# One-core attention, mixing and gated product on Trainium2: d's two halves as even and odd numbers

## The chip, the cores and the metric

The kernel runs on one core of a Trainium2 chip. The metric is the time of the whole program on the device, in microseconds (us). TensorE (PE) multiplies and writes to PSUM; each of its matrix products comes with a load of the stationary tile, which the profile lists as an engine of its own (PEld). VectorE (DVE), ScalarE (ACT) and GpSimd (POOL) do the elementwise work. SP's queue issues most DMAs, POOL's the others.

## The reference, cut to what matters

```python
# attention: u, v are (4, 3072, 256), z is (4, 3072, 64)
attn = np.maximum((z @ z.T) / S, 0) ** 2
x = u * (attn @ v)
# mixing with the row before, then a gated net of width 1024
x_prev = x shifted down by one row, zeros in the first
xk = mu_k * x + (1 - mu_k) * x_prev
xr = mu_r * x + (1 - mu_r) * x_prev
k = np.maximum(xk @ w_k, 0)
x = sigmoid(xr @ w_r) * (k * k @ w_v)
# a second gated product of width 1536
out = ((x @ w_a) * (x @ w_b)) @ w_out
```

The large weights come as float64, so the device reads them as pairs of 32-bit words and decodes them. mu_k and mu_r have one number for each of the 256 columns d of x.

## The kernel before

The program has three stages. In the first, attention, there are 24 blocks of 512 rows (4 batches of 6), and each is worked through in 12 pairs of key tiles. For a pair, two products make scores (`sc`, lines 461 and 462), ScalarE squares them (lines 474 and 475), or a block that was kept earlier is read back from DRAM (`pm`, line 506), since the scores are symmetric. Then the squared scores are split into a rounded part `hi` and a rest `lo` (lines 520, 522, 523). v is split in the same way into `vhi` and `vlo`. Three products per tile, `vhi*hi`, `vhi*lo` and `vlo*hi`, are summed in PSUM by `mm3` (lines 102 to 104) into two accumulators `acc[0]` and `acc[1]`, each of 128 columns of d by 512 rows. The inner function `bb` of `summed` picks v's stationary tile: `vh[:, k, c]` with `c = slice(d * P, (d + 1) * P)`, so half d holds columns 128 d to 128 d + 127, which lie side by side. Everything is in float32 or its rounded form for TensorE.

u is needed with d on the partitions. `u_load` (line 435) brings a block of 512 rows as 32-row squares in eight DMAs of 64 KB on SP's queue, each with runs of 32 numbers, and `u_prep` (line 441) turns the squares with one VectorE transpose for each half. `result` multiplies the accumulators by u, `change` and `mixed` make xk and xr, which go to DRAM for the second stage.

The second stage (`mixture1`) is the first gated net, by a scheme with seven products of half-size blocks in place of eight, and the third (`mixture2`) the second product by the same scheme. Weights are decoded during attention (`decode`), in steps that stand beside the attention's units; their rows are put on partitions by the views in `chunks` and `rows`.

The order is written out by hand: a list of units, and beside it a list of side steps with the number of the unit at which each stands (`at`). The u load of a block stands 4 units into the block, its two transposes 12 and 14 units in. In the second batch and after, v's parts come by GpSimd's DMAs (`v_parts`, lines 412 and 419): `vhi` is cast by the DMA, ScalarE writes its negative to `vlo` (line 416), and a second DMA adds v to that. Five pools of tiles hold the buffers; `ust`, `raw` and others share three (`stp`).

Of the kernel before, what the change touches and what calls it, by code (L numbers as in the profile page):

```python
# [8 lines left out]
F32 = mybir.dt.float32  # L9
# [6 lines left out]
P = 128  # L16
QB = 512
SQ = 32
# [10 lines left out]
def tile_kernel(  # L29
# [29 lines left out]
    nc = tc.nc  # L59
# [4 lines left out]
    ND = D // P  # L64
# [10 lines left out]
    stp = ctx.enter_context(tc.tile_pool(name="stp", bufs=3))  # L75
# [13 lines left out]
    mu = const.tile([P, 2, ND], F32, name="mu")  # L89
    edge = const.tile([P, ND], F32, name="edge")  # L90

    def g_tile(shape, dtype, name):
        return gp.tile(shape, dtype, tag="g", name=name)
# [7 lines left out]
    def mm3(ps, wh, wl, ah, al, first, last):  # L101
        nc.tensor.matmul(ps, wh, ah, start=first, stop=False)  # L102
        nc.tensor.matmul(ps, wh, al, start=False, stop=False)  # L103
        nc.tensor.matmul(ps, wl, ah, start=False, stop=last)  # L104
# [9 lines left out]
    def at(i, fn):  # L114
        sides.setdefault(max(i, 0), []).append(fn)
# [203 lines left out]
    def z_load(b, s, t=None, queues=()):  # L319


        if t is None:
            t = zp.tile([P, QB // SQ, SQ], F32, tag="zn", name="zn")
        for n in range(2):
            src = z[b, (s + n) * QB : (s + n + 1) * QB, :].rearrange("(b i) (a j) -> a i b j", i=SQ, j=SQ)
            for a in range(DK // SQ):
                c = n * DK + a * SQ
                (queues[a] if queues else nc.sync).dma_start(t[c : c + SQ], src[a])
        zn_t[b, s] = t

    def z_prep(b, s):

        n = s % 2
        h, l = (slice(m * DK, (m + 1) * DK) for m in (n, 1 - n))

        def turn():
            t = zt_t[b, s] = zt_t[b, s + 1] = ztp.tile([P, QB], F32, tag="zt", name="zt")
            raw = zn_t.pop((b, s)).rearrange("p b j -> p (b j)")
            if b or s:
                nc.vector.transpose(t, raw)  # L340
            else:
                nc.vector.transpose(t[:DK], raw[:DK])
                return lambda: nc.vector.transpose(t[DK:], raw[DK:])

        def high():
            kt_t[b, s] = ktp.tile([P, QB], F32R, tag="kt", name="kt")
            if b or s < 2:
                nc.scalar.activation(kt_t[b, s][h], zt_t[b, s][h], AF.Copy)
            else:
                nc.vector.tensor_copy(kt_t[b, s][h], zt_t[b, s][h])  # L350

        def low():
            nc.vector.tensor_tensor(kt_t[b, s][l], zt_t[b, s][h], kt_t[b, s][h].bitcast(F32), op=ALU.subtract)

        return turn, high, low
# [9 lines left out]
    def q_prep(b, s):  # L365


        def half(h):
            kt = kt_t[b, s].bitcast(F32)
            if h == 0:  # L370
                q_t[b, s] = g_tile([P, 2, QB], F32R, "q")
            q = q_t[b, s]
            m = h ^ s % 2
            k = turned_order(kt[m * DK : (m + 1) * DK])
            nc.vector.tensor_copy(by_order(q[0:DK, h, :]), k)
            nc.scalar.activation(by_order(q[DK : 2 * DK, h, :]), k, AF.Copy)

        return lambda: half(0), lambda: half(1)
# [6 lines left out]
    def v_load(s):  # L385
        vst_t[s] = g_tile([P, TPB, D], F32, "vst")
        nc.sync.dma_start(vst_t[s], v_rows(0, s))
# [34 lines left out]

    ust_t, ut_t = {}, {}

    def by_squares(rows, i):


        r = rows[i * QB : (i + 1) * QB, :]
        return r.rearrange("(b i) (h a j) -> a i h b j", i=SQ, h=ND, j=SQ)

    def u_load(i):
        t = stp.tile([P, ND, QB // SQ, SQ], F32, tag="st", name="ust")
        for d in range(ND):
            for a, src in enumerate(by_squares(u.rearrange("b s d -> (b s) d"), i)):
                nc.sync.dma_start(t[a * SQ : (a + 1) * SQ, d], src[:, d])
        ust_t[i] = t

    def u_prep(i, d):
        if d == 0:
            ut_t[i] = g_tile([P, ND, QB], F32, "ut")  # L440
        nc.vector.transpose(ut_t[i][:, d, :], ust_t[i][:, d].rearrange("p b j -> p (b j)"))

    early_z = []
    x_kept, p_kept = {}, {}
# [1 line left out]
    def attention(i):  # L446
        b, qb = divmod(i, NQB)
        base = len(units)
        acc = {}
# [46 lines left out]
        def mirrored(kb, pr):  # L496

            st = {}

            def load():  # L500
                if pr:
                    return
                m = pm_t[kb] = pmp.tile([P, TPB, TPB, P], F32, tag="pm", name="pm")
                rows = p_kept[b, qb, kb].rearrange("(a q) (g c) t i -> g q a (c t i)", q=SQ, g=TPB)
                for g in range(TPB):
                    nc.sync.dma_start(m[g * SQ : (g + 1) * SQ].rearrange("q a c r -> q a (c r)"), rows[g])

            def a():
                st["p"] = halves(pm_t[kb][:, :, 2 * pr : 2 * pr + 2, :].rearrange("p a t r -> p t a r"), True)

            return st, a, load
# [14 lines left out]
        def summed(st, kb, pr, first, last):  # L526
            def bb():
                if first:
                    for d in range(ND):
                        acc[d] = accp.tile([P, QB], F32, tag="acc", name="acc")  # L530
                hi, lo = st["p"]
                vh, vl = v_t[b, kb]
                for t in range(2):
                    k = 2 * pr + t
                    for d in range(ND):
                        c = slice(d * P, (d + 1) * P)
                        mm3(
                            acc[d], vh[:, k, c], vl[:, k, c], hi[:, t, :], lo[:, t, :],
                            first and t == 0, last and t == 1,
                        )  # L540

            return bb

# [37 lines left out]
        for n, fn in enumerate(steps):  # L581
            t = base + NKT + (2 * AHEAD + 3 * n + 3 if i < NB - 1 else n + 4)
# [4 lines left out]
        if qb == 0:  # L587
            for s in range(0 if b else 1, NQB):
                need = base + s * TPB
                turn, high, low = z_prep(b, s)  # L590
                if b:
                    w = base - 16 + (s - NQB + 2) * NKT - 8 * (s < NQB - 1)
# [24 lines left out]
        for n, (_, m, kb, pr) in enumerate(order):  # L617
            if m:
                st, a, load = mirrored(kb, pr)
                at(base + 2 * n - 9, load)  # L620
            else:
                st, a = scored(kb, pr, base + 2 * n)
# [758 lines left out]
    n2 = len(units)  # L1381
    mixture2()

    chunks = [(("r", 0), 0, w_r.rearrange("(k p) d -> p k d", p=P))]
    def by_rows(name, w, g):
        wr = w.rearrange("(n t p) d -> n p t d", p=P, t=2)
        for h in range(2):
            chunks.append(((name, g), h * QB, wr[2 * g + h]))
# [3 lines left out]
    place = iter([  # L1392
        (DEC1 if b else DEC0) + n * DEC + b * NQB * NKT for b in range(B) for n in range(PER if b else PER - 1)
    ])
    rows = {n: w.rearrange("(k p) f -> k p f", p=P) for n, w in (("a", w_a), ("b", w_b), ("k", w_k))}
    groups = [("s", (g,), ("b", g), ("a", g)) for g in range(NF2 // TPB)] + [("k", (), ("k", 1), ("k", 0))]
    for kind, g, low_rows, high_rows in groups:
        val = {}
# [14 lines left out]
        i = next(place)  # L1413
# [30 lines left out]
    with tc.manual_schedule():  # L1444
        z_load(0, 0, None, (nc.sync, nc.scalar))
        zs = g_tile([P, 2, QB // SQ, SQ], F32, "zs")
        z_load(0, 2, zs[:, 0])
        v_load(0)
        z_load(0, 4, zs[:, 1])
        for n in range(1, NQB):  # L1450
            v_load(n)
        for c, m in enumerate((mu_k, mu_r)):
            nc.sync.dma_start(mu[:, c, :], m.rearrange("(d p) -> p d", p=P))
        turn, high, low = z_prep(0, 0)
        turn_next = turn()
        for fn in (high, low, *q_prep(0, 0), turn_next, *early_z[0]):
            fn()
        for n, fn in enumerate(v_split(0)):
            at(n // 2, fn)
        last = max(len(units), max(sides) + 1)  # L1460
        for i in range(last):
            if i == n1:
                while pending:
                    pending.popleft()()
                early.close()
                late["ps"] = ctx.enter_context(
                    tc.tile_pool(name="psp", bufs=4, space=bass.MemoryType.PSUM, reuse_waits="tile")
                )
                late["w"] = ctx.enter_context(tc.tile_pool(name="wp", bufs=6, reuse_waits="tile"))
                late["p"] = ctx.enter_context(tc.tile_pool(name="late", bufs=18, reuse_waits="tile"))  # L1470
            for fn in sides.get(i, ()):
                fn()
            if i < len(units):
                a, b, ahead = units[i]
                if a is not None:
                    a()
                if b is not None:
                    pending.append(b)
            else:
                ahead = 0  # L1480
            while len(pending) > ahead:
                pending.popleft()()
# [27 lines left out]
```

## Time and profile before

| | before |
|---|---|
| median of 3 runs (range) | 2548.71 us (2547.96 to 2548.97) |
| the profiled execution, its own time | 2548.83 us |
| its span, first to last instruction | 2546.9 us |
| PE busy | 2529.3 us, 11128 products |
| PEld busy | 2089.4 us, 11128 loads |
| DVE busy | 2055.2 us |
| ACT busy | 1848.8 us |
| DMA | 335842 packets, 495.22 MB; 189056 packets under 512 B |

A product's mean duration in the profile, near 390 ns, runs from the issue to the modelled end, and products overlap in it. What each costs in a dense stretch is the distance from one start to the next, or the count of products over the length of a stretch. Attention takes the first 950 us or so, the second stage some 500 us, the third the rest.

### The profile page before, as it was taken

To read this page: it belongs to the slowest core of one execution; us is meant where nothing else is said; L and a number is where in the kernel's file an instruction comes from. 1 tells how busy PE (TensorE), PEld (TensorE's weight loads), DVE (VectorE), ACT (ScalarE), POOL (GpSimd) and SP (SyncE) were. 2 spreads that over 40 slices of the span, in tenths; PEclk is the share of its full clock that TensorE was granted. 3 is DMA by queue.
4 is the path that set the end of the run, shared out by engine and by line. 5 is a ranking of instruction groups with operands and counts; after the bars stand their busy time and mean duration, and the time that the engine had idled before them with its cause. 6 is when DMAs were issued, how large, how long until landed. Compare 5 with 4: busy or idle time off the path is not lost.

```text
span 2546.9 us, 32165 instructions
## 1 busy us (share of the span) xinstructions
PE 2529.3 (99%) x11128; PEld 2089.4 (82%) x11128; DVE 2055.2 (81%) x2879; ACT 1848.8 (73%) x2519; POOL 372.2 (15%) x382
## 2 busy tenths in 40 slices
PE   8999999999999999999999999999999999999999
PEld 6887888888888888888888888888888888888887
DVE  9997999799979886666666668888888888888887
ACT  7865987687687758888888876666666666666665
POOL 0111211210120100000000002222222222212211
PEclk9999999999999999999999999999999999999999
DMA  8789888997997793112122146666766676666664
GB/s 215 223 234 237 261 252 232 249 281 224 243 257 233 227 264 141 67 58 92 50 75 75 50 144 245 194 235 199 240 196 231 212 223 207 223 227 217 213 194 137
DMA packets 335842, 495.22 MB, mean 194 GB/s; under 512 B 189056, under 2 KB 211584, under 8 KB 328000
## 3 DMA queue, kind: packets, MB, share of 16 engines
q1 hardware_dynamic: 293232, 362.75, 49.4%
q0 software_dynamic: 40848, 129.77, 15.7%
q8 instruction: 87, 1.43, 0.2%
q10 hardware_dynamic: 1600, 0.66, 0.1%
q14 instruction: 75, 0.61, 0.1%
HBM read 357.04 MB, written 136.05 MB: 194 GB/s over the span
## 4 chain that ended last, share of the span: by engine, by line
PE 94%; DVE 2%; issue 1%; DMA 1%; ACT 1%; POOL 0%; SPq 0%; DVEq 0%; POOLq 0%
PE px L992 15%; PE acc L103 9%; PE acc L104 9%; PE acc L102 9%; PE py L992 8%; PE px L715 5%; PE oacc L1023 4%; PE oacc L1021 4%; PE oacc L1022 4%; PE pw L992 4%; PE vacc L102 3%; PE vacc L104 3%; PE vacc L103 3%; PE py L715 3%; PE sc L461 2%; PE sc L462 2%
## 5 line engine op out<-in xcount | busy, mean ns | idle before, releaser
L103 PE MATMUL acc<-lo,vhi 128*128 128x512 f32 x1152 | 449.3, 390 | 1.4 <-DVE lo L523 1.4
L102 PE MATMUL acc<-hi,vhi 128*128 128x512 f32 x1152 | 449.1, 390 | 0.8 <-DVE hi L522 0.8
L104 PE MATMUL acc<-hi,vlo 128*128 128x512 f32 x1152 | 448.9, 390 | 0.0
L992 PE MATMUL px<-t,sw 128*128 128x512 f32 x1296 | 364.1, 389 | 0.0
L992 PEld LDWEIGHTS px<-t,sw 128*128 128x128 f32 x1296 | 243.2, 188 | 50.7 <-DVE cc L1177 0.3
L103 PEld LDWEIGHTS acc<-lo,vhi 128*128 128x128 f32 x1152 | 216.7, 188 | 48.0 <-DVE lo L523 2.9
L102 PEld LDWEIGHTS acc<-hi,vhi 128*128 128x128 f32 x1152 | 216.6, 188 | 46.3 <-DVE hi L522 1.2
L104 PEld LDWEIGHTS acc<-hi,vlo 128*128 128x128 f32 x1152 | 216.6, 188 | 44.8
L1077 ACT ACTIVATE pw<-px 128x512 f32<-128x512 f32 x144 | 83.8, 582 | 197.8 <-PE px L992 197.8
L474 ACT ACTIVATE p<-sc 128x1024 f32<-128x1024 f32 x167 | 169.6, 1016 | 57.2 <-PE sc L462 56.5
L1189 POOL TENSOR_TENSOR cc<-cc 128x512 f32<-128x512 f32 x72 | 93.1, 1293 | 804.8 <-DVE b L1043 581.8
L523 DVE TENSOR_TENSOR lo<-p,hi 128x1024 fp32r<-128x1024 f32 x167 | 199.5, 1195 | 4.2
L1089 DVE TENSOR_TENSOR u<-py,u 128x512 f32<-128x512 f32 x144 | 99.5, 691 | 124.8 <-PE py L992 124.8
L475 ACT ACTIVATE p<-p 128x1024 f32<-128x1024 f32 x167 | 177.3, 1062 | 5.3
L481 DVE STREAM_TRANSPOSE pt<-p 128x512 f32<-128x512 f32 x240 | 155.5, 685 | 28.9 <-ACT p L475 27.5
L523 DVE TENSOR_TENSOR lo<-pm,hi 128x1024 fp32r<-128x1024 f32 x120 | 145.7, 1215 | 27.8 <-ACT hi L520 27.6
L1132 ACT ACTIVATE c<-pw 128x512 f32<-128x512 f32 x144 | 86.4, 600 | 111.0 <-PE pw L992 81.3
L520 ACT ACTIVATE hi<-pm 128x1024 fp32r<-128x1024 f32 x120 | 124.4, 1050 | 45.5 <-DMA pm<-pkept 35.1
L1187 POOL TENSOR_TENSOR cc<-cc 128x512 f32<-128x512 f32 x71 | 91.8, 1293 | 438.9 <-DVE bl L1043 218.3
L102 PE MATMUL vacc<-kh,w 128*128 128x512 f32 x384 | 149.4, 389 | 0.0
L104 PE MATMUL vacc<-kh,w 128*128 128x512 f32 x384 | 149.4, 389 | 0.0
L103 PE MATMUL vacc<-kl,w 128*128 128x512 f32 x384 | 149.4, 389 | 0.0
(213 smaller groups left out, 6051.2 us busy)
## 6 DMA issues: line engine op xcount, KB each, us to landing
sw<-kept SPq DMA_DIRECT2D x252, 512.0 KB, 5.5
pkept<-pt POOLq DMA_DIRECT2D x60, 1024.0 KB, 6.0
pm<-pkept SPq DMA_DIRECT2D x240, 256.0 KB, 6.6
ow<-kept SPq DMA_DIRECT2D x120, 512.0 KB, 6.7
kept<-w POOLq DMA_DIRECT2D x42, 512.0 KB, 5.4
ust<-in_u SPq DMA_DIRECT2D x192, 64.0 KB, 5.7
xkept<-xr POOLq DMA_DIRECT2D x24, 512.0 KB, 7.0
xkept<-xk POOLq DMA_DIRECT2D x24, 512.0 KB, 6.3
```

Of the source, the lines that this page charges most:

```text
L102: nc.tensor.matmul(ps, wh, ah, start=first, stop=False)
L103: nc.tensor.matmul(ps, wh, al, start=False, stop=False)
L104: nc.tensor.matmul(ps, wl, ah, start=False, stop=last)
L474: nc.scalar.activation(p, sc, AF.Relu, scale=1.0 / S)
L475: nc.scalar.activation(p, p, AF.Square)
L481: nc.vector.transpose(pt[:, :, 2 * pr + t, :], p[:, t, :].rearrange("p (c i) -> p c i", i=SQ))
L520: nc.scalar.activation(h, p, AF.Copy)
L523: nc.vector.tensor_tensor(l, p, h.bitcast(F32), op=ALU.subtract)
L715: nc.tensor.matmul(bank, w[x][:, c], t[:, y, :], start=first and m == 0, stop=end and m == 2, skip_group_check=True)
L992: nc.tensor.matmul(bank, w, t[:, y, :], start=first and m == 0, stop=end and m == 2, skip_group_check=True)
L1021: nc.tensor.matmul(acs[bank], wh, hi, start=first, stop=False, skip_group_check=True)
L1022: nc.tensor.matmul(acs[bank], wl, hi, start=False, stop=False, skip_group_check=True)
```

## The change

Half d of the 256 columns was columns 128 d to 128 d + 127; it is now the columns 2 j + d, so half 0 holds the even and half 1 the odd ones. Four things follow.

- u's block is loaded in four DMAs of 128 KB with runs of 64 numbers (256 bytes) in place of eight with runs of 32, and the transposes of a half read every second number of `ust`.
- v's stationary tiles `vh` and `vl` are read by TensorE with a stride of two numbers. v itself is stored as before.
- mu's view is `(p d)` in place of `(d p)`.
- The rows of w_r and w_k are put on partitions as `(p k)` in place of `(k p)`, so that a partition has the two neighbouring rows.

The products, the VectorE, ScalarE and GpSimd instructions and their order are the same, row for row; on SP's queue the u loads have four DMAs each. The shapes of mu's two loads and of w_r's one change too. On SP, at the start of the program (`vst` is v, `ust` u, `zn` z, `pm` kept scores), before:

```order
L387 DMA vst<-in_v 128x4x256 x5
L1453 DMA mu<-in_moe_mu_k 128x2x1
L1453 DMA mu<-in_moe_mu_r 128x2x1
L435 DMA ust<-in_u 32x16x32 x8
L328 DMA zn<-in_z 32x16x32 x4
L506 DMA pm<-pkept 32x4x512 x4
```

and with the change:

```order
L387 DMA vst<-in_v 128x4x256 x5
L1444 DMA mu<-in_moe_mu_k 128x2
L1444 DMA mu<-in_moe_mu_r 128x2
L429 DMA ust<-in_u 32x16x64 x4
L328 DMA zn<-in_z 32x16x32 x4
L499 DMA pm<-pkept 32x4x512 x4
```

What stood behind a u load stands behind four DMAs in place of eight, and nothing changes places.

```diff
-    def by_squares(rows, i):
-        r = rows[i * QB : (i + 1) * QB, :]
-        return r.rearrange("(b i) (h a j) -> a i h b j", i=SQ, h=ND, j=SQ)
-
     def u_load(i):
-        t = stp.tile([P, ND, QB // SQ, SQ], F32, tag="st", name="ust")
-        for d in range(ND):
-            for a, src in enumerate(by_squares(u.rearrange("b s d -> (b s) d"), i)):
-                nc.sync.dma_start(t[a * SQ : (a + 1) * SQ, d], src[:, d])
-        ust_t[i] = t
+        t = ust_t[i] = stp.tile([P, QB // SQ, ND * SQ], F32, tag="st", name="ust")
+        r = u.rearrange("b s d -> (b s) d")[i * QB : (i + 1) * QB]
+        for a, src in enumerate(r.rearrange("(b i) (a c) -> a i b c", i=SQ, c=ND * SQ)):
+            nc.sync.dma_start(t[a * SQ : (a + 1) * SQ], src)
 
     def u_prep(i, d):
         if d == 0:
             ut_t[i] = g_tile([P, ND, QB], F32, "ut")
-        nc.vector.transpose(ut_t[i][:, d, :], ust_t[i][:, d].rearrange("p b j -> p (b j)"))
+        nc.vector.transpose(ut_t[i][:, d, :], ust_t[i].rearrange("p b (j h) -> p h b j", h=ND)[:, d])
...
                     for d in range(ND):
-                        c = slice(d * P, (d + 1) * P)
-                        mm3(
-                            acc[d], vh[:, k, c], vl[:, k, c], hi[:, t, :], lo[:, t, :],
-                            first and t == 0, last and t == 1,
-                        )
+                        h, l = (x[:, k, :].rearrange("p (c h) -> p h c", h=ND)[:, d] for x in (vh, vl))
+                        mm3(acc[d], h, l, hi[:, t, :], lo[:, t, :], first and t == 0, last and t == 1)
...
-    chunks = [(("r", 0), 0, w_r.rearrange("(k p) d -> p k d", p=P))]
+    chunks = [(("r", 0), 0, w_r.rearrange("(p k) d -> p k d", p=P))]
...
-    rows = {n: w.rearrange("(k p) f -> k p f", p=P) for n, w in (("a", w_a), ("b", w_b), ("k", w_k))}
+    rows = {n: w.rearrange("(k p) f -> k p f", p=P) for n, w in (("a", w_a), ("b", w_b))}
+    rows["k"] = w_k.rearrange("(p k) f -> k p f", p=P)
...
-            nc.sync.dma_start(mu[:, c, :], m.rearrange("(d p) -> p d", p=P))
+            nc.sync.dma_start(mu[:, c, :], m.rearrange("(p d) -> p d", p=P))
```

## Rows read from the trace of the kernel before

**Rows 1.** The page: busy time by engine; granted TensorE clock and DMA in slices.
```profile
PE 2529.3 (99%) x11128; PEld 2089.4 (82%) x11128; DVE 2055.2 (81%) x2879; ACT 1848.8 (73%) x2519; POOL 372.2 (15%) x382
PEclk9999999999999999999999999999999999999999
DMA  8789888997997793112122146666766676666664
```
**Rows 2.** PE's waits: who waited for whom, us in total, times, longest.
```profile
PE sc L461 <- DVE q L375: 6.4, 1, 6.4
PE sc L461 <- ACT p L474: 3.2, 2, 2.4
PE acc L103 <- DVE lo L523: 1.4, 2, 0.8
PE acc L102 <- DVE hi L522: 0.8, 1, 0.8
```
**Rows 3.** Stretches of the span: busy us (instructions) of PE, PEld, DVE, ACT, POOL; clock, DMA.
```profile
100.00:200.00 100.00, 100.00 (x443) 82.84 (x442) 94.09 (x141) 72.51 (x82) 11.10 (x18) 1.00 0.86 233
200.00:300.00 100.00, 97.58 (x430) 80.47 (x430) 78.68 (x114) 73.09 (x78) 21.00 (x25) 1.00 1.11 252
...
1800.00:2300.00 500.00, 500.00 (x2207) 414.17 (x2206) 419.12 (x572) 334.75 (x537) 118.20 (x93) 1.00 0.66 216
```
**Rows 4.** Groups by line: count, busy us, mean ns, idle before. Products, then loads.
```profile
L103 PE MATMUL acc<-lo,vhi 128*128 128x512 f32 x1152 | 449.3, 390 | 1.4 <-DVE lo L523 1.4
...
L103 PEld LDWEIGHTS acc<-lo,vhi 128*128 128x128 f32 x1152 | 216.7, 188 | 48.0 <-DVE lo L523 2.9
```
**Rows 5.** Timeline at 249 us, attention: start, duration in us; products, then loads.
```profile
249.01 0.39 PE L102 MATMUL acc<-hi,vhi 128*128 128x512 f32 x1
249.24 0.39 PE L103 MATMUL acc<-lo,vhi 128*128 128x512 f32 x1
...
249.01 0.19 PEld L103 LDWEIGHTS acc<-lo,vhi 128*128 128x128 f32 x1
249.24 0.19 PEld L104 LDWEIGHTS acc<-hi,vlo 128*128 128x128 f32 x1
```
**Rows 6.** Timeline at 20 us, where the clock is low for a while.
```profile
20.48 0.63 PE L104 MATMUL acc<-hi,vlo 128*128 128x512 f32 x1
20.90 0.63 PE L102 MATMUL acc<-hi,vhi 128*128 128x512 f32 x1
...
20.48 0.33 PEld L102 LDWEIGHTS acc<-hi,vhi 128*128 128x128 f32 x1
```
**Rows 7.** The transposes at the end (moving side 128 columns): timeline; durations min/median/max in ns.
```profile
2540.32 0.36 PEld L1344 LDWEIGHTS pt<-one,ot 128*128 128x128 f32 x3
...
L1344 PEld LDWEIGHTS pt<-one,ot x16: 138/140/143, 2539.2 to 2540.9; 128*128 128x128 f32 x16
```
**Rows 8.** Groups on DVE, as in rows 4.
```profile
L182 DVE TENSOR_SCALAR e<-raw 128x512 uint32<-128x512 uint32 x27 | 11.3, 418 | 0.2
...
L470 DVE CAST hi<-p 128x512 fp32r<-128x512 f32 x2 | 0.8, 420 | 0.0
...
L441 DVE STREAM_TRANSPOSE ut<-ust 128x512 f32<-128x512 f32 x48 | 33.9, 705 | 0.6
```
**Rows 9.** Timelines of 225 to 256 us: SP's queue, ACT, PE; idle before in brackets.
```profile
225.20 17.01 SPq L435 DMA_DIRECT2D ust<-in_u  x8
...
250.94 1.06 ACT L416 ACTIVATE vlo<-vhi 128x1024 fp32r<-128x1024 f32 x1 [5.12 <-DMA vhi<-in_v]
...
252.96 0.50 PE L461 MATMUL sc<-q,kt 128*128 128x512 f32 x1 [2.42 <-ACT p L474]
```
**Rows 10.** u's DMAs; SP's queue in 13:60, then 1130:1230: packets, MB, share of 16 engines.
```profile
ust<-in_u SPq DMA_DIRECT2D x192, 64.0 KB, 5.7
...
q1 hardware_dynamic: 13998, 5.90, 58.7%
...
q1 hardware_dynamic: 2752, 6.29, 18.0%
```

## The prediction

> **What bounds the kernel now.** I read the page's busy times first, then PE's waits, then stretches by count of products, and last single products and loads. PE is busy for 2529.3 of the span's 2546.9 us, at a granted clock that shows nine tenths or more in all forty slices [rows 1]. Busy alone proves little, since products overlap in the record, so the count decides: 443 products in 100 us of attention, 2207 in 500 us of the third stage [rows 3]. That is 225.7 and 226.6 ns from one start to the next in two stages whose other engines and DMAs are loaded quite differently (a DMA share of 0.86 and 0.66). So the spacing is PE's own, and 11128 products at 226.6 ns make 2521.6 us of the span.
>
> What is left for others to give back is small. PE's waits with a releaser sum to 6.4 + 3.2 + 1.4 + 0.8 = 11.8 us [rows 2]. 6.4 is the start, before the first operand is there. Of the rest, the single wait of 0.8 for `hi` and the longest, 0.8, of the two for `lo` come before 20 us; what stays later is the 3.2 us for ScalarE's `p` and 0.6 us for `lo`, 3.8 us in all. The largest single piece is a hole of 2.42 us that ends at 252.96 us [rows 9]. The stretch 200 to 300 us shows it: 430 products where 443 fit, 13 x 226 ns = 2.9 us [rows 3].
>
> **The change part by part.** *v's stationary tiles.* It touches the loads of lines 102 to 104 in attention: 3 x 1152 = 3456 of them, each 188 ns, each beside a product [rows 4]. Only the load's reading changes; the product's moving side stays contiguous. A load starts with the product before its own (both at 249.01, then both at 249.24) [rows 5] and is followed by (48.0 - 2.9) us / 1152 = 39 ns in which the load side has nothing to do [rows 4]. So a load may grow by 39 ns before anything is late. How much of a load is reading is seen in the transposes at the end, which move only 128 columns and so don't hide their loads: three loads of 140 ns stand in 0.36 us, hence (360 - 140) / 2 = 110 ns from one to the next at full clock [rows 7]. No row shows TensorE reading with a stride. The nearest row is VectorE: `raw` is read in every second 32-bit word at line 182, 418 ns for 512 words, and the contiguous cast of 512 float32 at line 470 takes 420 ns [rows 8]. That stride costs nothing there, at VectorE's faster rate of the two in these rows. By this row the cost is 0; at the other end, with reading at half the rate, a load takes 188 + 110 = 298 ns, 298 - 188 - 39 = 71 ns too long, and 3456 x 0.071 = 245 us. A gain is excluded: the spacing of 226 ns is the same with contiguous tiles everywhere, and a stride takes no work away. I take 0, the value of the nearest row, and price the other end as a rival.
>
> [...]
>
> *u's loads.* 192 DMAs of 64 KB become 96 of 128 KB, and a block's 8 x 512 = 4096 packets of 128 bytes become 2048 of 256. The price of a packet I fit to two stretches of SP's queue [rows 10]: 13998 packets of 421 bytes in the mean took 58.7% of 16 engines for 47 us, 441 us or 31.5 ns each; 2752 of 2286 bytes took 18.0% for 100 us, 288 us or 104.7 ns each. That is 0.039 ns a byte, so 20 ns at 128 bytes and 25 ns at 256, an estimate. A block's u takes 4096 x 20 / 16 = 5.1 us of all engines now and 2048 x 25 / 16 = 3.2 us then: 1.9 us less, 24 times, 46 us of DMA time. Nearly all of it is hidden under PE's products. Where it isn't is the hole at 250 us: SP is occupied for 17.01 us from 225.20 with one u load, against a median of 5.7 us to landing for such a DMA, in a stretch where the DMA queues together show 1.11 of 16 engines; ScalarE's negative of v then waits 5.12 us for `vhi`'s DMA, and the scores' `p` behind it on ScalarE holds PE for 2.42 us [rows 3, 9, 10]. I take 1.9 us of these 2.42 back. The bounds are a gain of all 3.8 us and a loss of 2.4 us, another hole of that size, since the kept scores, z and raw weights behind u on SP's queue now start sooner and may meet v's DMAs elsewhere.
>
> *u's transposes.* 48 of 705 ns, now reading with a stride of two [rows 8]. Taken at 0 by line 182's row; at the other end they double, 48 x 0.705 = 34 us of VectorE work (priced below). The cover is VectorE's idle time: 5.9 us in the stretch 100 to 200, 21 us in 200 to 300 [rows 3]. Each half's first transpose now needs four DMAs that bring both halves, not its own four; the load stands eight units ahead, which is more than the landing time.
>
> *mu, w_r, w_k, and the waits.* Two loads of 1 KB, one of 512 KB and four of 512 KB keep their places and sizes; w_r's runs become longer. What waits for them is decoding and mixing far behind on VectorE and ScalarE. 0, with 0.5 us either way.
>
> The sum: 2548.83 (the profiled execution, 0.12 above the median) + 0 - 1.9 + 0 + 0 = 2546.9 us.
>
> **The rivals.** *The load becomes the bound.* It decides once a strided load takes over 188 + 39 = 227 ns. For it: the load cannot start before the product ahead of it does, so a longer load shows at once [rows 5]. Against it: line 182's row, and even at half rate 220 ns from load to load would still fit in 227 if only the rate counted. Price up to 245 us, 2546.9 + 245 = 2792 us; slower. Chance 0.10.
>
> [...] Chance 0.08.
>
> *VectorE becomes late.* If the strided transposes take twice as long, some of the 34 us come through where VectorE is full: about half of the 24 blocks, 0.7 us each, 8 us, 2555 us. PE waited for VectorE only 0.6 us after 20 us, so the cover is mostly there. Chance 0.04.
>
> *The DMAs give back more than PE's recorded waits.* A gain of over 0.2% is 5.1 us, more than the 3.8 us that PE loses after 20 us; it would need a shorter start too, which u has no part in. 2543 us, chance 0.02.
>
> *The larger packets do nothing* (SP's DMAs still collide with v's): 2548.8 us. This lies within the forecast.
>
> **How the numbers follow.** The forecast, strided reading free and a small relief of the DMAs, has 0.76, between 2545 (all 3.8 us back) and 2551.3 (a second hole). 0.2% is about what a measurement of this kernel can tell from no change, so it counts as the same. Slower is 0.10 + 0.08 + 0.04 = 0.22, faster 0.02, the same 0.76. The range of 2543 to 2556 us takes in the forecast, the faster case and VectorE's, 0.82 less a little at the forecast's own edges; the two TensorE rivals are left out.
>
> **What would show it.** Right: the loads of lines 102 to 104 still at 188 ns, 443 products in 100 us of attention, the u transposes at 705 ns, packets under 512 bytes down from 189056 by some 49000, and a shorter hole near 250 us. [...] The forecast is wrong if the spacing in attention is no longer that of the third stage.

## The result: 0.8% slower, in the products with v

| | before | after |
|---|---|---|
| median (range) | 2548.84 us (2547.96 to 2550.35) | 2568.53 us (2568.1 to 2568.68) |
| ratio, 95% interval | | 1.0076 (1.0059 to 1.0094) |
| span of the profiled execution | 2546.9 us | 2566.9 us |

The changed kernel's page begins with the busy time by engine, and further down gives the packets:

```profile
PE 2551.4 (99%) x11128; PEld 2108.9 (82%) x11128; DVE 2056.7 (80%) x2879; ACT 1850.1 (72%) x2519; POOL 372.5 (15%) x382
...
DMA packets 284770, 495.21 MB, mean 193 GB/s; under 512 B 138112, under 2 KB 160640, under 8 KB 276928
...
ust<-in_u SPq DMA_DIRECT2D x96, 128.0 KB, 7.5
```

PE's waits after the change (who waited for whom, us in total, times, longest):

```profile
PE sc L454 <- DVE q L375: 6.4, 1, 6.4
PE acc L102 <- DVE hi L515: 1.1, 1, 1.1
PE acc L103 <- DVE lo L516: 1.0, 2, 0.8
PE sc L454 <- ACT p L461: 0.3, 1, 0.3
PE acc L103 <- DVE lo L464: 0.2, 1, 0.2
PE sc L454 <- DVE kt L353: 0.2, 1, 0.2
```

Two stretches by engine (PE, PEld, DVE, ACT, POOL; then clock and DMA), one of attention and one of the third stage:

```profile
100.00:200.00 100.00, 100.00 (x431) 82.94 (x430) 91.03 (x136) 71.81 (x81) 10.79 (x17) 1.00 0.85 225
...
1800.00:2300.00 500.00, 500.00 (x2208) 414.32 (x2207) 418.52 (x573) 333.42 (x534) 118.19 (x93) 1.00 0.67 220
```

And groups of the products with v, their loads and u's transposes (count, busy us, mean ns, idle before):

```profile
L103 PE MATMUL acc<-lo,vhi 128*128 128x512 f32 x1152 | 455.5, 395 | 1.5 <-DVE lo L516 1.0 <-DVE lo L464 0.2
...
L103 PEld LDWEIGHTS acc<-lo,vhi 128*128 128x128 f32 x1152 | 223.1, 194 | 49.2 <-DVE lo L516 4.1 <-DVE lo L464 0.5
...
L434 DVE STREAM_TRANSPOSE ut<-ust 128x512 f32<-128x512 f32 x48 | 33.9, 706 | 2.3 <-DMA ust<-in_u 1.2 <-issue 0.8
```

Read against [rows 2 to 4, 8, 10]: the third stage runs as before, 2208 products for 2207. Attention at the full clock runs 431 products where 443 ran, with PE busy for all 100 us of both. PE doesn't wait more; it waits less, 9.2 us in all for 11.8, and the hole of 2.4 us is gone. The loads of v's tiles grew by only 6 ns, from 188 to 194, and still have their idle time of near 40 ns each, and nonetheless every product came later. The transposes are as fast as they were.

Between 600 and 950 us, where PE waits for nothing in either kernel, the count gives the size (all lines, columns as above):

```profile
600.00:950.00 350.00, 350.00 (x1546) 289.93 (x1545) 308.03 (x460) 252.40 (x284) 45.07 (x66) 1.00 0.91 238
...
600.00:950.00 350.00, 350.00 (x1507) 290.17 (x1506) 305.44 (x459) 255.51 (x287) 45.47 (x67) 1.00 0.88 233
```

The first line is before, the second after: 350 / 1545 = 226.5 ns and 350 / 1506 = 232.4 ns from start to start. 1279 of the 1507 are products with v; put down to them alone, each costs (232.4 - 226.5) x 1506 / 1279 = 6.9 ns more. Read one by one in the trace, the starts of successive products with v stand 233.3 ns apart in this stretch, 226.7 before, so 6.7 ns. The scores' products between them, whose own tiles lie side by side in both kernels, come a little later as well (228.0 ns from one to the next, 226.7 before). At 6.7 ns, the size that the products alone show below too, 3456 products make 23.2 us; less the 2.6 us that PE waits less, 20.6 us, for a difference of spans of 20.0 us.

### The profile page after: what moved, and what is told of

Same layout as the page of the kernel before. It is cut to its first block, busy times and chain, and to the rows that moved or that the text cites. A ratio compares the mean times of both kernels' runs of the same rounds, so it can differ in the third digit from the quotient of the medians.

```text
span 2566.9 us, 32030 instructions
## 1 busy us (share of the span) xinstructions
PE 2551.4 (99%) x11128; PEld 2108.9 (82%) x11128; DVE 2056.7 (80%) x2879; ACT 1850.1 (72%) x2519; POOL 372.5 (15%) x382
## 3 DMA queue, kind: packets, MB, share of 16 engines
q0 software_dynamic: 40848, 129.77, 15.5%
## 4 chain that ended last, share of the span: by engine, by line
PE 95%; DVE 2%; issue 1%; DMA 1%; SPq 0%; POOL 0%; ACT 0%; DVEq 0%; POOLq 0%; ACTq 0%
PE px L982 15%; PE acc L103 9%; PE acc L104 9%; PE acc L102 9%; PE py L982 8%; PE px L705 5%; PE oacc L1013 4%; PE oacc L1011 4%; PE oacc L1012 4%; PE pw L982 4%; PE vacc L102 3%; PE vacc L104 3%; PE vacc L103 3%; PE py L705 3%; PE sc L455 3%; PE sc L454 3%
## 5 line engine op out<-in xcount | busy, mean ns | idle before, releaser
L103 PE MATMUL acc<-lo,vhi 128*128 128x512 f32 x1152 | 455.5, 395 | 1.5 <-DVE lo L516 1.0
L102 PE MATMUL acc<-hi,vhi 128*128 128x512 f32 x1152 | 454.8, 395 | 1.1 <-DVE hi L515 1.1
L104 PE MATMUL acc<-hi,vlo 128*128 128x512 f32 x1152 | 454.7, 395 | 0.0
L103 PEld LDWEIGHTS acc<-lo,vhi 128*128 128x128 f32 x1152 | 223.1, 194 | 49.2 <-DVE lo L516 4.1
L102 PEld LDWEIGHTS acc<-hi,vhi 128*128 128x128 f32 x1152 | 223.2, 194 | 47.4 <-DVE hi L515 1.5
L104 PEld LDWEIGHTS acc<-hi,vlo 128*128 128x128 f32 x1152 | 223.1, 194 | 45.4
```

## Experiments

### One half of the change each: u_only, v_only

u_only is the changed kernel with v's tiles side by side again; u's loads and transposes and the views of mu, w_r and w_k stay changed:

```diff
-                        h, l = (x[:, k, :].rearrange("p (c h) -> p h c", h=ND)[:, d] for x in (vh, vl))
-                        mm3(acc[d], h, l, hi[:, t, :], lo[:, t, :], first and t == 0, last and t == 1)
+                        c = slice(d * P, (d + 1) * P)
+                        mm3(
+                            acc[d], vh[:, k, c], vl[:, k, c], hi[:, t, :], lo[:, t, :],
+                            first and t == 0, last and t == 1,
+                        )
```

> The changed kernel with v's stationary tiles read side by side again, as before; u's 256-byte packets, the strided transposes and the other views stay, so that the halves of d no longer match and the product with u mixes columns. If the strided loads are the whole loss: about 2546.5 us, between 2545 and 2548.7, loads of lines 102 to 104 back at 188 ns and 443 products in 100 us of attention. If u's loads or the strided transposes have part in the loss: over 2551 us.

Measured: 2552.76 us against 2549.32, ratio 1.0009 (1.0000 to 1.0018). The signs of the first case came back, 443 products in 100 us and loads of 188 ns:

```profile
100.00:200.00 100.00, 100.00 (x443) 82.81 (x442) 94.17 (x141) 72.82 (x82) 11.39 (x18) 1.00 0.87 234
...
L104 PEld LDWEIGHTS acc<-hi,vlo 128*128 128x128 f32 x1152 | 216.2, 188 | 44.6
```

Its time did not: the median lies over the 2551 us that stood for a part of u in the loss. Against the kernel before, run beside it, the difference is 0 to 4.6 us by the interval. So a small part of the 20 us may belong to what u_only keeps changed, and a gain of 1.9 us isn't there.

v_only is the kernel before with this edit the other way round: v's tiles with a stride of two, nothing else.

> The kernel before with v's stationary tiles read with a stride of two, nothing else, so that the halves of d no longer match u's. If the strided loads are the whole loss: 3456 loads x 6 ns = 21 us, 2569 to 2570 us, a little over the changed kernel since the hole near 250 us stays. If u has part in it: under 2560 us.

Measured: 2568.15 us against 2549.32, ratio 1.0071 (1.0057 to 1.0085): the loss of the whole change, within the intervals. Between 600 and 950 us it runs the same 1507 products as the changed kernel, and its PE waits keep the hole (2.5 us for `p`), as expected:

```profile
600.00:950.00 350.00, 350.00 (x1507) 289.31 (x1506) 305.69 (x460) 254.16 (x286) 45.52 (x67) 1.00 0.89 234
...
PE sc L461 <- ACT p L474: 2.5, 1, 2.5
```

The stride of v's stationary tiles is the cause of the loss.

This run also shows strided tiles at the lower clock: the granted clock was 0.50 from 19.2 to 22.4 us. There the products stand 0.42 to 0.43 us apart, as they do without a stride [rows 6], so no cost of the stride shows at that clock:

```profile
19.54 0.63 PE L104 MATMUL acc<-hi,vlo 128*128 128x512 f32 x1
19.97 0.63 PE L102 MATMUL acc<-hi,vhi 128*128 128x512 f32 x1
20.39 0.63 PE L103 MATMUL acc<-lo,vhi 128*128 128x512 f32 x1
```

u_only also shows where the relief of the DMAs went. SP's queue is done with the u load at 225 us in 5.79 us, not 17.01 [rows 9]; these are the rows of its timeline (SP, then ACT), and of its PE waits:

```profile
225.46 5.79 SPq L429 DMA_DIRECT2D ust<-in_u  x4
...
234.42 7.25 SPq L328 DMA_DIRECT2D zn<-in_z  x4
...
243.38 1.06 ACT L416 ACTIVATE vlo<-vhi 128x1024 fp32r<-128x1024 f32 x1 [7.16 <-DMA vhi<-in_v]
...
PE sc L454 <- ACT p L467: 2.5, 3, 1.2
...
PE sc L454 <- DVE kt L353: 1.3, 2, 0.7
```

The raw weights and z behind u are now issued into the same stretch (z at 234 us instead of 243), ScalarE's longest wait for `vhi` is 7.2 us instead of 5.1 (35.6 us in all, 23.6 before), and PE's one hole of 2.4 us became several smaller ones, with a new one behind z's tile `kt`. VectorE waits 2.1 us for u's DMAs, which it never did. After 20 us PE waits 4.8 us, 3.8 before. That it is z and the weights that `vhi` now waits for is likely from these times; no run takes them away to show it.

### How the cost goes with the stride: v_four, strides

v_four reads v's tiles with a stride of four:

```diff
-                        c = slice(d * P, (d + 1) * P)
-                        mm3(
-                            acc[d], vh[:, k, c], vl[:, k, c], hi[:, t, :], lo[:, t, :],
-                            first and t == 0, last and t == 1,
-                        )
+                        h, l = (
+                            x.rearrange("p t d -> p (t d)").rearrange("p (g c h) -> p g h c", g=2, h=4)[:, k // 2, 2 * (k % 2) + d]
+                            for x in (vh, vl)
+                        )
+                        mm3(acc[d], h, l, hi[:, t, :], lo[:, t, :], first and t == 0, last and t == 1)
```

> The kernel before with v's stationary tiles read with a stride of four numbers, so that tiles hold the wrong columns. Theory 1, a fixed charge for a strided load: 2569 us as with a stride of two. [...]

Measured: 2576.22 us, ratio 1.0104 (1.0090 to 1.0118). That is 27 us, some 7 or 8 more than the fixed charge asks and than a stride of two costs, though its loads last 310 ns:

```profile
L104 PE MATMUL acc<-hi,vlo 128*128 128x512 f32 x1152 | 457.1, 397 | 0.0
L104 PEld LDWEIGHTS acc<-hi,vlo 128*128 128x128 f32 x1152 | 356.7, 310 | 0.0
```

A load of 310 ns whose product comes 235 ns after the one ahead: loads overlap each other, so it is their rate that counts, not their length. The forecast's reading by the rate holds in the main (the table below has 233 ns, not 220, which doesn't quite fit into 227), and the reading by length (245 us) is out.

strides is products alone, in a loop for each kind (two of the 19 loops; R is 200):

```diff
...
+    for _ in range(R):
+        nc.tensor.matmul(acc[:P, :512], tile_of(2), moving(512), start=True, stop=True)
+    for _ in range(R):
+        nc.tensor.matmul(acc[:P, :512], tile_of(3), moving(512), start=True, stop=True)
...
```

> Products alone, 200 of each kind one after the other on tiles that stay, no other work; nothing of the reference is computed. [...] With 256 moving columns: +5.8 again if the charge comes once for each load whatever moves; 0 if it comes from the moving side's reading being kept waiting only near the end of a long product. With 128 moving columns, where loads are 110 ns apart: 116 at a stride of two if a strided load merely reads 6 ns longer; 220 if it reads at half the rate and the long product hides the rest.

The timeline has a line for each kind (start, duration), and the spacing is the next kind's start less its own, over 200; strides 1, 2, 3, 4, 8:

```profile
56.24 45.50 PE L66 MATMUL acc<-m,w 128*128 128x512 f32 x200
...
101.58 46.83 PE L68 MATMUL acc<-m,w 128*128 128x512 f32 x200
...
148.25 47.27 PE L70 MATMUL acc<-m,w 128*128 128x512 f32 x200
...
195.35 47.16 PE L72 MATMUL acc<-m,w 128*128 128x512 f32 x200
...
242.36 49.23 PE L74 MATMUL acc<-m,w 128*128 128x512 f32 x200
```

All spacings worked out in this way, in ns (stationary tiles of 128 columns but for the second line):

```
stride of the tile            1      2      3      4      8
512 moving columns        226.7  233.4  235.5  235.1  245.3
512, tiles of 64 columns  230.0  231.2         233.3
256 moving columns        120.0  120.0         233.4
128 moving columns        111.4  117.8         233.4  240.0
```

The bottom line is the load's own rate: 111 ns for 128 numbers side by side, 118 at a stride of two, 233 at four. So a stride of two is nearly as fast as none, and a stride of four half as fast; 235 ns at 512 columns and a stride of four is then nearly the load as the bound. But for a stride of two the rate explains nothing: 118 ns is little more than half a product of 512 columns, and at 256, where it just fits into 120, the stride costs nothing at all. With tiles of 64 columns the stride costs 1.2 ns, where the fixed charge asks for 232.4 - 226.6 = 5.8; and such tiles, side by side, cost 3.3 ns more than whole ones. A fixed charge gives neither. Why the load's rate is halved at a stride of four and not at two, no run shows.

### What else costs 6 ns: strides_2, vlo_only

> Products alone again, 200 of each kind, nothing of the reference computed. In the first table a tile with a stride of two cost 6.6 ns at 512 moving columns, 0 at 256, 6 at 128 (where the load itself is the bound), and a side-by-side tile of 64 columns cost 3.3 ns. Theory A, the load's reads hold up the moving side's reads: 6.6 ns shrinks in proportion to the moving columns, about 5.8 at 448, 5 at 384, 4 at 320. Theory B, a fixed charge once the load is done well before the product ends: 6.6 at 448, 384 and 320 too, 0 only where load and product end together; then side-by-side tiles of 32, 96, 112 and 120 columns, whose loads end earlier still, cost something too. Theory C, the address at which the tile begins: an offset of one or two numbers costs a side-by-side tile something, and an odd offset changes the strided tile's spacing. At 192 moving columns, spacing 80 + 13 = 93 ns if the load's 112 ns were no bound; 112 and 118 if they are. Strided and side-by-side loads in turn: half the charge, 230, if it is paid for each strided load; 226.7 if only strided loads in a row pay.

In ns, by the same working (with 512 moving columns where nothing else is said; the last line from the starts of single products, after one with a tile side by side and after one with a stride):

```
side by side, begins at number 0, 1, 2      226.7  232.4  230.7
stride of two, begins at number 0, 1        233.3  233.4
side by side, 32, 96, 112, 120 columns      231.7  230.0  229.0  233.4
448 moving columns, stride 1, 2             206.6  203.4
384                                         173.5  173.4
320                                         146.7  146.7
192                                         111.6  118.8
strides 1 and 2 in turn                     231.2  235.7
```

A tile without any stride that begins one number later costs 5.7 ns; one of 120 columns, with less to read, 6.7; at 448 moving columns the strided tile is the faster one. Theories A and B fall with 384 and 320, where a stride costs nothing. Theory C holds for tiles side by side and not for strided ones, which cost the same from either address. The last line says that the charge isn't the strided load's own: where every second load is strided, all products pay, 4.5 and 9.0 ns.

vlo_only is the same in the whole kernel, the stride for a third of the loads:

```diff
-                        c = slice(d * P, (d + 1) * P)
+                        h = vh[:, k, d * P : (d + 1) * P]
+                        l = vl[:, k, :].rearrange("p (c h) -> p h c", h=ND)[:, d]
```

> The kernel before with the stride of two for vlo's tiles alone, 1152 of the 3456 loads, so that vlo's part goes to the wrong columns. If every strided load is charged by itself: a third of the loss, 1152 x 5.7 ns = 6.6 us, about 2555.5 us. If a charge comes only where strided loads follow one another: 2549 us. If one strided load in a group of three disturbs the group as much as three: 2568 us.

Measured: 2561.25 us against 2549.81, ratio 1.0047 (1.0031 to 1.0064). A third of the loads brings over half of the loss, 11 us where 6.6 were expected by the load, some 10 ns for each strided load. All three products of a group pay: between 600 and 950 us the next one starts 230.3, 230.0 and 232.4 ns after those of lines 102, 103 and 104, where it was 226.7 each before. Together that is 12.6 ns a group, some 15 us in all; the profiled executions differ by 12.7 us, and the one before lost some 2.5 us more to PE's waits and to its stretch at the lower clock (0.54 granted from 19.2 to 22.4 us) [rows 6]. The loads at lines 102 and 103 are 188 ns long, as before, yet their products' mean in the record is 393 ns, not 390:

```profile
L103 PE MATMUL acc<-lo,vhi 128*128 128x512 f32 x1152 | 452.5, 393 | 1.7 <-DVE lo L523 1.3 <-DVE lo L471 0.2
...
L103 PEld LDWEIGHTS acc<-lo,vhi 128*128 128x128 f32 x1152 | 216.5, 188 | 55.4 <-DVE lo L523 4.4 <-DVE lo L471 0.5
```

### No stride at all: v_offset, strides_3

By then I held that the loss has to do with how load and product fit together in time, and that the stride is only one way to disturb it. Two runs could refute that. v_offset is the kernel before, with tiles that begin at an odd number:

```diff
-                        c = slice(d * P, (d + 1) * P)
+                        c = slice(1 + 126 * d, 1 + 126 * d + P)
```

> The kernel before, v's tiles side by side as there, but each beginning at an odd number (columns 1 to 128 and 127 to 254), so that most sums go to a neighbouring column; no stride anywhere. If the loss is a matter of strided reading: 2549 us, loads at 188 ns. If it is a matter of how the load's and the product's timing fit together, for which a one-number offset was as bad as a stride in the table (232.4 ns against 226.7): 3456 x 5.7 ns = 20 us, 2568 to 2570 us, with loads that last 188 ns as before.

Measured: 2569.98 us against 2548.21, ratio 1.0086 (1.0069 to 1.0103). Contiguous tiles, loads of 188 to 190 ns, and the loss of the whole change (22 us; the intervals overlap):

```profile
600.00:950.00 350.00, 350.00 (x1504) 282.82 (x1504) 305.23 (x462) 254.66 (x287) 45.48 (x67) 1.00 0.88 234
...
L103 PEld LDWEIGHTS acc<-lo,vhi 128*128 128x128 f32 x1152 | 219.2, 190 | 54.6 <-DVE lo L523 1.1
L104 PEld LDWEIGHTS acc<-hi,vlo 128*128 128x128 f32 x1152 | 216.3, 188 | 48.6
```

So a loss of this size needs no strided reading. That a stride and an odd address cost the same for the same reason is not shown by it.

> Products alone, 200 of each kind, nothing of the reference computed: 512 moving columns and then fewer in steps, each with a side-by-side tile and one with a stride of two. Theory of the fit in time: what a product's spacing has over its columns at 2.4 GHz moves between 13 and 20 ns as the columns change, for both kinds, and at some widths the strided tile is the cheaper one (at 448 it was, 203.4 against 206.6). Theory of strided reading: the strided tile is 6.6 ns dearer, or as dear, at every width, and 448 was a chance reading that doesn't come back.

Measured, in ns:

```
moving columns   512    508    504    500    496    488    480    464    448    432
stride 1       226.7  227.7  226.7  226.7  220.0  225.6  216.7  210.0  202.7  195.8
stride 2       233.3  226.7  226.7  226.6  225.3  220.0  216.6  211.7  203.4  193.3
```

The strided tile is dearer at 512, 496, 464 and 448, cheaper at 508, 488 and 432, and as dear at the others. 448 didn't come back as it was: the tile side by side took 202.7 ns here and 206.6 in strides_2, the strided one 203.4 in both, so differences under 4 ns between two single rows prove little. The one at 488 (5.6 ns in favour of the stride) and the one at 512 (6.7 ns against it, in all three runs) are beyond that. The columns themselves go at 2.4 to a ns by strides, at the full clock: 512 take 226.7 ns and 256 take 120.0, so 256 more cost 106.7. What a product has over its columns at that rate goes from 13.3 ns (432, stride 2; 512, stride 1) to 22.3 (488, stride 1). Side by side, widths of 500, 504 and 512 cost the same 226.7, though 12 columns are 5 ns. These rows of the timeline show it:

```profile
55.35 45.50 PE L63 MATMUL acc<-m,w 128*128 128x512 f32 x200
100.68 46.83 PE L65 MATMUL acc<-m,w 128*128 128x512 f32 x200
147.35 45.70 PE L67 MATMUL acc<-m,w 128*128 128x508 f32 x200
...
328.90 45.49 PE L75 MATMUL acc<-m,w 128*128 128x500 f32 x200
374.23 45.49 PE L77 MATMUL acc<-m,w 128*128 128x500 f32 x200
419.56 44.16 PE L79 MATMUL acc<-m,w 128*128 128x496 f32 x200
463.56 45.22 PE L81 MATMUL acc<-m,w 128*128 128x496 f32 x200
```

Many of the spacings lie on steps of 6.67 ns: 120.0, 146.7, 173.4, 220.0, 226.7 and 233.3 are 18, 22, 26, 33, 34 and 35 of them. Others lie between (210.0, 216.7, 225.6). A product of 512 columns with a tile of 128 numbers side by side from number 0 takes 34 such steps, with a stride of two 35. But it is not that each product takes whole steps: at 464 columns, side by side, single starts are 205 and 215 ns apart in turn, and neither is a whole number of them. That the chip has such a step, and what makes it, no run shows; why the spacing grows stays open. What is shown is that a loss of this size doesn't need the stride, that the stride's loss isn't in proportion to the strided loads, and that it comes and goes with the product's width.

## Why the prediction was wrong

The predicted time was 2546.9 us, the measured one 2568.53, outside the range of 2543 to 2556. The prediction's own sign of being wrong came: the spacing in attention is no longer that of the third stage.

- **What bounds the kernel** was right: the spacing of PE's products is the kernel's time, and the loss is 3456 products at some 6.7 ns.
- **The step that failed** is "So a load may grow by 39 ns before anything is late". The idle time behind each load was taken for slack. The load grew by 6 ns, well inside it, and the product came 6.7 ns later. The 39 ns are no reserve, whatever fills them, which stays open: v_offset's products came as late with loads that hardly grew at all. The rate of 110 ns [rows 7] was read rightly (111 in strides) and says when the load itself is the bound; it says nothing on the spacing below that.
- **The value 0 for the strided load**, taken from VectorE's row, was off by 6.7 ns for each product. Another engine's row showed what strided reading costs there. It could not show how a load sits between two products. The bounds (0 to 245 us) held the 23 us, but between ends so far apart the range should not have closed at 2556.
- **The rivals.** The first (a load over 227 ns) was out; v_four's loads are that long and cost 27 us, not 245. No run shows what the 0.08 in the sum for slower stands for; in its place the runs showed 6.7 ns a product at 512 moving columns, with loads of 194 ns for 188, only in attention and, by v_only's start, only at the full clock, and no cost of the stride at 256, 320 and 384 columns. The transposes did cost nothing (706 ns for 705).
- **u's loads.** The term of -1.9 us failed too, in a size that hardly counts. The hole did close in the changed kernel, but v_only, with u's loads as they were, keeps it, and u_only, with the new loads and contiguous tiles, has smaller ones instead and is 0 to 4.6 us slower. What stood behind u on SP's queue moved into the same stretch, which the forecast had only as a bound. The packets fell by 50944, near the 49000 forecast. The relief of the queue did not come near the 46 us of the fit: it was busy for 49.4% of 2546.9 us before and 48.8% of 2549.0 in u_only, 14 us of all engines, and even that is no more than the spread of the runs that leave u's loads alone (1244 us in vlo_only, 1259 in v_four). In the trace a packet of 128 bytes on this queue took 15.5 ns in the mean before, and one of 256 bytes 25.3 ns in u_only, where the fit had 20 and 25; so one large packet costs little less than the two small ones that it replaces.

## What to carry to other kernels

Where products stand back to back and PE is the bound, anything that touches a stationary tile's address pattern (stride, first address, number of columns) can move the spacing, by 2 to 7 ns a product of 512 columns in these runs, even if the load stays far shorter than the product: price it by a loop of that very product, with its width and its tile, and don't take the load's idle time for slack. A stride of two for a stationary tile is cheap at the load (118 ns for 111) and a stride of four halves its rate (233); whether the product sees it depends on its width. And DMAs that are made cheaper in a stretch where the queues are full let others in (in u_only z was issued at 234 us, not 243, and ScalarE's longest wait for `vhi` was 7.2 us, not 5.1); look at what stands behind them before a wait is counted as gone.

## What the hardware showed unasked

- A *moving* side with a stride of two runs at half the rate. In strides, from 670 to 846 us at the full clock, 389 products with 512 such columns took 176 us, 453 ns each for 226.7 side by side:

```profile
670.00:846.00 176.00, 176.00 (x389) 81.78 (x388) 0.00 (x0) 0.00 (x0) 0.00 (x0) 1.00 0.00 0
```

- With a stationary stride of four or eight and only 128 moving columns, where PE stands in the record as busy all the time but the spacing is the load's, the granted clock fell to 0.50 (second line), and the 233 ns at a stride of four stayed as they were at a granted clock of 1.00 with 256 columns (first line):

```profile
478.00:524.00 46.00, 46.00 (x200) 46.00 (x200) 0.00 (x0) 0.00 (x0) 0.00 (x0) 1.00 0.00 1
...
600.00:617.00 17.00, 17.00 (x74) 17.00 (x74) 0.00 (x0) 0.00 (x0) 0.00 (x0) 0.50 0.00 0
```
